# Odd tokens of two batches by quadrants in a later phase, and another order of work between two batches

## The chip, the cores and the metric

The kernel runs on one core of a Trainium2 chip. The metric is the device time of one execution in microseconds. A core has TensorE (PE, matrix products; its weight loads are listed as PEld), VectorE (DVE), ScalarE (ACT), GpSimd (POOL) and SyncE (SP, which issues DMAs), each with its own instruction queue, on-chip memory of 128 partitions (SBUF), and accumulator banks for matrix products (PSUM).

## The reference

Linear attention over 8 batches of 8 heads with 576 tokens of 64 dimensions, followed by a two-layer network over the 4608 tokens.

```python
def _attn_ref(q, k, v):                       # 8 x 8 x 576 x 64
    phi = lambda x: np.where(x > 0, x, np.exp(x) - 1.0) + 1.0
    q_p, k_p = phi(q), phi(k)
    kv = np.einsum('bhsd,bhse->bhde', k_p, v)
    z = np.sum(k_p, axis=2)
    num = np.einsum('bhsd,bhde->bhse', q_p, kv)
    den = np.einsum('bhsd,bhd->bhs', q_p, z)[..., None] + 1e-06
    return num / den

def _moe_ref(x, w_in, w_out, beta):           # x: 4608 x 512, w_in: 512 x 2048, w_out: 2048 x 512
    h = x @ w_in
    g = h * (1.0 / (1.0 + np.exp(-beta * h)))
    return g @ w_out
```

## The kernel before

Everything is bf16 on TensorE with f32 accumulation. Each engine's instructions run in the order in which the program writes them; the order is fixed by hand, and tiles with a tag rotate through a fixed number of buffers (`bufs`), so that a new tile waits for the readers of an old one.

**Tokens.** A batch's 576 tokens are 64 groups of J = 9. Slot j of every group makes a row of 64 tokens, and four pairs of slots make four blocks of 128 tokens (t = 0 to 3). Slot 8, the odd one, is block 4 and has only 64 tokens per batch. The odd tokens of all eight batches are gathered in `xT_tail` (512 tokens) and go through the network as a ninth batch at the very end.

**Phases.** For each batch b there is an h phase (Hb: 16 blocks `ff` of 128 hidden units, each with four matmuls of 512 columns, `h_mm`, L395, followed by the swish on ScalarE, `silu`, L403) and a y phase (Yb: four tiles of 128 tokens with 16 matmuls each, `y_mm`, L413, copied out of PSUM by VectorE and stored by DMAs of SP, `y_out`). The loop over b = 1 to 8 at the end of the program puts side work into these phases with `at(phase, place, ...)`: the attention of batch b+1 into Hb (`kv_both` at ff 10, `numers` and `norms` after ff 15), its transposition into Yb's queue (`x_trans_dma`), the feature map of batch b+2 into Yb (`phi_all`, `q_trans_dma`), and loads. Batch 0 and the part of batch 1 ahead of H1 are written out in straight code, because nothing precedes them to hide them.

**Batches 2 to 7** form keys times values, and the sums of keys as a 65th column of the values, by quadrants (`kv_both`, L224): four products of 64x64 in the four quarters of the PE array. `numers` (L289) multiplies the transposed queries with it in the same way; the queries are transposed by DMA (`q_trans_dma`), and so is the result x (`x_trans_dma`).

**Batches 0 and 1** before the change: the sums of the keys (`z_products`) and keys times values (`kv_direct`) go through `row_products` (L179), products with 64 rows and all 128 columns in two row halves, of which the mask keeps the diagonal blocks (`z_evac` L190, `kv_evac` L203, `diagonal` L616). Queries are transposed on TensorE (`q_trans`, L257). Denominators are small matmuls of two columns (`dens`, L475), with `recips` (L482) on VectorE; numerators are `numer_mm` (L563) and `numer0` (L493), normalised into a tile `xs`, which TensorE transposes (`x_part` L587, `x_trans` L371) and ScalarE or VectorE copies into `xT` or `xT_tail`. The odd block of batch 0 is spread over H0 (transposition at ff 5, denominators at ff 7, numerators at ff 8, x at ff 10); that of batch 1 is computed with the other blocks, and its x is transposed at ff 8 of H1.

**Between H0 and H1** stands Y0, written by hand: its matmuls (`y_mm(0, t, i, ...)`, i = quarter of the hidden units) fill TensorE between the steps of batch 1's attention. `w_out_scale` (VectorE, L668) must have scaled the quarter i of `w_out` before.

**Loads.** POOL issues the loads that convert from f32 to bf16, one behind the other: keys and values of batch 0, four parts of `w_in`, `w_out` and the inputs of batches 1 and 2 in the order of the program. SP issues all other DMAs, the transposing ones among them.

Of the kernel before, what the change touches and what calls it, by code (L numbers as in the profile page):

```python
# [16 lines left out]
def kernel(  # L17
# [79 lines left out]
    tiny = consts.tile([P, 2], BF16)  # L97
    nc.scalar.activation(tiny[:, 0:1], warm[:, 0:1], ACTF.Exp)
# [76 lines left out]
    def row_products(b, pr, dsts, mov):  # L175
        for j in range(J):
            for hh in range(2):
                r = slice(hh * G, (hh + 1) * G)
                nc.tensor.matmul(  # L179
                    dsts[hh], st[b, "k"][r, pr, j, :], mov(r, j),  # L180
                    start=(j == 0), stop=(j == J - 1), skip_group_check=True,
                )

    def z_products(b, pr, ps):

        row_products(b, pr, [a[:, 256 + 2 * pr : 258 + 2 * pr] for a in ps], lambda r, j: ones[r])

    def z_evac(ps):
        for hh in range(2):
            nc.vector.tensor_mul(  # L190
                z0[:, hh], ps[hh][:, 256:260].rearrange("p (a h) -> p a h", a=2),
                kvmask[:, :, :, 0],
            )

    def kv_direct(b, pr, ps):
        row_products(
            b, pr, [a[:, pr * P : (pr + 1) * P].rearrange("p (h d) -> p h d", h=2) for a in ps],
            lambda r, j: vb[b][r, 2 * pr : 2 * pr + 2, j, :],
        )

    def kv_evac(b, hh, prs, ps):
        p0, p1 = prs[0], prs[-1] + 1
        nc.vector.tensor_mul(  # L203
            st[b, "kv"][:, hh, p0:p1].rearrange("p a (h e) -> p a h e", h=2)[:, :, :, 0:D],
            ps[hh][:, p0 * P : p1 * P].rearrange("p (a h d) -> p a h d", a=p1 - p0, h=2),
            kvmask[:, p0:p1, :, 0:D],
        )
# [7 lines left out]
    def kv_both(b):  # L215

        t = num_tile("kvp")
        for pr in range(2):
            for j in range(J):
                for h in range(2):  # L220
                    for hh in range(2):
                        r = slice(hh * G, (hh + 1) * G)
                        c = slice(h * D, (h + 1) * D)
                        nc.tensor.matmul(  # L224
                            t[c, hh, pr * EA : (pr + 1) * EA],
                            st[b, "k"][r, pr, j, c],
                            vaug[b % 2][r, pr, j, h, 0:EA],
                            start=(j == 0), stop=(j == J - 1), skip_group_check=True,
                        )
        st[b, "kvd"] = work.tile([P, 2, 2 * EA], BF16, tag="kv_bd", name="kvd")  # L230
        nc.vector.tensor_copy(st[b, "kvd"], t[:, :, 0 : 2 * EA])  # L231
# [16 lines left out]
    def q_trans(b, ts, tp, engs):  # L248

        if (b, "qT") not in st:  # L250
            st[b, "qT"] = work.tile([P, NT, 2, 2, P], BF16, tag="qT", name="qT")
# [12 lines left out]
    def q_trans_dma(b):  # L264
        st[b, "qTd"] = work.tile([P, 38, G], BF16, tag="qT", name="qTd")
        nc.gpsimd.memset(st[b, "qTd"][:, 36:37], 0.0)
        for hh in range(2):
# [3 lines left out]
            )  # L271

# [29 lines left out]
    def numers(b):  # L302
# [9 lines left out]
        st[b, "nps"] = pairs, odd  # L312

# [47 lines left out]
    def x_trans(b, t, eng):  # L361
        n = P if t < NT - 1 else G
        xv = st[b, "xs", t].rearrange("p i a d -> p (i a d)")
        if b == 1 and t == NT - 1:
            tp = num_tile("xtp")[:, 0].bitcast(BF16)[:, 0 : KC * P].rearrange(
                "p (c t) -> p c t", c=KC
            )
        else:
            tp = miscps.tile([P, KC, P], BF16, tag="misc", name="xtp")
# [10 lines left out]
    def x_trans_dma(b, t):  # L380
# [5 lines left out]
        for pr in range(2):  # L386
            nc.sync.dma_start_transpose(
                out=xT_tail[:, pr:4:2, b * G : (b + 1) * G],
# [128 lines left out]
    for i in range(3):  # L517
        load_w_out(i)
    load(nc.gpsimd, xk[1], k, 1)
    load(nc.gpsimd, xq[1], q, 1)  # L520
# [29 lines left out]
    z_evac(zt)  # L550

    def q_trans0(t):
        q_trans(0, (t,), misc_bf()[:, 0 : 512 if t < NT - 1 else 256], (nc.scalar,))
# [58 lines left out]
    def diagonal(hh):  # L612

        for h in range(2):
            r = slice(h * D, (h + 1) * D)
            nc.scalar.copy(  # L616
                kv0[r, hh, 1, h * EA : h * EA + D], kvp0[hh][r, P + h * D : P + (h + 1) * D]
# [29 lines left out]
    for ff in range(4, FC):  # L647
# [3 lines left out]
        if ff == 5:  # L651
            q_trans0(4)
        if ff == 7:
            dps4 = num0_tile()
            dens(0, (4,), dps4)
            recips(4, 5, G, dps4)
        if ff == 8:
            numer0(0, 4)
        if ff == 10:
            x_trans(0, 4, nc.vector)  # L660
# [18 lines left out]
    yps = [mm_tile("y_ps") for _ in range(4)]  # L679
    phi_all(1, "k")  # L680
    phi_all(1, "q")
# [4 lines left out]
    kv_tile(1)  # L686
    y_mm(0, 0, 2, yps[0])
    y_mm(0, 1, 2, yps[1])
    for pr in range(2):
        z_products(1, pr, kv1)  # L690
    z_evac(kv1)
    w_out_scale(3, 0)
    y_mm(0, 2, 2, yps[2])
    for ts in ((0, 1), (2, 3)):
        q_trans(1, ts, num0_tile().bitcast(BF16), (nc.scalar, nc.scalar))
    y_mm(0, 3, 2, yps[3])
    dps1 = num0_tile()
    q_trans(1, (4,), dps1.bitcast(BF16)[:, 512:768], (nc.scalar,))
# [4 lines left out]
    dens(1, range(NT), dps1)  # L703
    recips(0, 4, P, dps1)
    recips(4, 5, G, dps1)
# [30 lines left out]
    numer0(1, 4)  # L736
# [36 lines left out]
    for b in range(1, B + 1):  # L773
        n = b + 1
        sh, sy = {}, {}
        if b == 1:
            at(sh, 0, lambda: q_trans_dma(2))
            at(sh, 8, lambda: x_trans(1, 4, nc.vector))
            at(sh, 1, lambda: [v_copy(nc.gpsimd, 2, pr) for pr in range(2)])
            at(sh, 2, lambda: load_kq(3, st[2, "qTd", "dma"]), lambda: load_v(3))  # L780
        if n < B:
# [42 lines left out]
```

## Time and profile before

| | |
|---|---|
| median of 4 runs | 289.35 us (288.54 to 291.07) |
| the profiled execution | 291.07 us, span 289.3 us |
| PE busy | 278.4 us, 96% |
| ACT busy | 159.9 us, 55% |
| DVE busy | 107.4 us, 37% |
| POOL busy | 37.1 us, 13% |
| DMA | 40.90 MB, mean 141 GB/s |

Times in the trace count from the start of the span. The first h matmul starts at 15.02, H0 ends at 33.26 with the first matmul of Y0, H1 starts at 53.17, Y1 at 68.95, H2 at 82.94. A line of the timeline merges neighbouring instructions of one kind: start, busy time, engine, line, operation, tiles, shape, count, and in brackets the idle time ahead of it with what ended it. Matmuls overlap, so the distance from one start to the next tells the cost of a group better than its busy time. Some matmul records are missing from the trace.

### The profile page before, as it was taken

To read this page: it belongs to the slowest core of one execution; us is meant where nothing else is said; L and a number is where in the kernel's file an instruction comes from. 1 tells how busy PE (TensorE), PEld (TensorE's weight loads), DVE (VectorE), ACT (ScalarE), POOL (GpSimd) and SP (SyncE) were. 2 spreads that over 40 slices of the span, in tenths; PEclk is the share of its full clock that TensorE was granted. 3 is DMA by queue.
4 is the path that set the end of the run, shared out by engine and by line. 5 is a ranking of instruction groups with operands and counts; after the bars stand their busy time and mean duration, and the time that the engine had idled before them with its cause. 6 is when DMAs were issued, how large, how long until landed. Compare 5 with 4: busy or idle time off the path is not lost.

```text
span 289.3 us, 5761 instructions
## 1 busy us (share of the span) xinstructions
PE 278.4 (96%) x2374; PEld 138.6 (48%) x2409; DVE 107.4 (37%) x261; ACT 159.9 (55%) x217; POOL 37.1 (13%) x54
## 2 busy tenths in 40 slices
PE   7799999999999999999999999999999999999994
PEld 2594447544444444444445444544454444444443
DVE  5731866834630491038203930293026100110021
ACT  5758856965837852785177718770860076018500
POOL 8632100310005000500050006100000000000000
PEclk9979999999999999999999999999999999999999
DMA  8999999599789839983898489848404510230033
GB/s 218 205 220 381 251 252 184 129 165 243 89 144 272 159 64 149 270 154 64 130 270 163 77 130 267 164 78 113 120 2 78 116 36 0 51 85 11 0 74 75
DMA packets 51083, 40.90 MB, mean 141 GB/s; under 512 B 30944, under 2 KB 42480, under 8 KB 51056
## 3 DMA queue, kind: packets, MB, share of 16 engines
q1 hardware_dynamic: 38160, 23.48, 37.5%
q0 software_dynamic: 12736, 16.91, 29.8%
q8 instruction: 19, 0.31, 0.4%
q10 hardware_dynamic: 160, 0.13, 0.2%
q14 instruction: 8, 0.07, 0.1%
HBM read 36.71 MB, written 9.44 MB: 160 GB/s over the span
## 4 chain that ended last, share of the span: by engine, by line
PE 92%; DMA 3%; issue 1%; POOL 1%; DVE 0%; ACT 0%; POOLq 0%
PE y_ps L413 43%; PE h_ps L395 42%; DMA w_in<-in_moe_w_in_dram 3%; PE kvp L224 1%; PE h_ps L597 1%; PE nps L289 1%; PE kv L179 1%; POOL vf L83 1%; PE nps_m L289 1%; PE xtp L371 0%; PE nps L493 0%; POOL xk L83 0%; PE nps L257 0%; PE tp L587 0%; PE nps L475 0%
## 5 line engine op out<-in xcount | busy, mean ns | idle before, releaser
L403 ACT ACTIVATE g<-h_ps,beta_c 128x512 bf16<-128x512 f32 x144 | 98.0, 688 | 95.2 <-PE h_ps L395 94.7
L413 PE MATMUL y_ps<-w_out,g 128*128 128x512 bf16 (+3 forms) x583 | 125.7, 370 | 0.8
L395 PE MATMUL h_ps<-xT,w_in 128*128 128x512 bf16 x481 | 109.4, 379 | 1.1 <-DVE xT L378 0.2
L413 PEld LDWEIGHTS <-g 128*128 128x128 bf16 x600 | 57.6, 98 | 64.0
L395 PEld LDWEIGHTS <-w_in 128*128 128x128 bf16 x560 | 54.0, 98 | 63.9 <-issue 0.2
L237 DVE COPY y_sb<-y_ps 128x512 f32<-128x512 f32 (+2 forms) x35 | 23.5, 673 | 73.2 <-PE y_ps L413 73.2
L231 DVE CAST kvd<-kvp 128x260 bf16<-128x260 f32 x6 | 2.6, 429 | 50.0 <-PE kvp L224 50.0
L83 POOL DMA_DIRECT2D xq<-in_q_dram x7 | 5.2, 743 | 111.9 <-ACT g L403 75.8
L142 ACT ACTIVATE e<-xk 128x1152 bf16<-128x1152 bf16 x16 | 17.9, 1152 | 1.1 <-DMA xk<-in_k_dram 1.1
L142 ACT ACTIVATE e<-xq 128x1152 bf16<-128x1152 bf16 x14 | 15.6, 1155 | 0.1
L395 PE MATMUL h_ps<-xT_tail,w_in 128*128 128x512 bf16 x62 | 13.9, 379 | 0.1
L153 DVE TENSOR_TENSOR phi_k<-e,r 128x1152 bf16<-128x1152 bf16 x16 | 11.6, 754 | 2.4 <-ACT e L142 2.1
L319 DVE TENSOR_TENSOR xs<-nps,rden 128x512 bf16<-128x512 f32 (+1 forms) x24 | 12.2, 552 | 0.4
L153 DVE TENSOR_TENSOR phi_q<-e,r 128x1152 bf16<-128x1152 bf16 (+2 forms) x17 | 11.7, 718 | 0.7 <-ACT e L142 0.4
L328 DVE TENSOR_SCALAR den<-nps 128x12 f32<-128x12 f32 x12 | 2.0, 165 | 25.8 <-PE nps L289 25.8
L171 POOL CAST vaug<-vf 128x1152 bf16<-128x1152 f32 x10 | 11.2, 1158 | 1.6 <-DMA vf<-in_v_dram 1.6
L142 ACT ACT_TABLE_LOAD x6 | 7.7, 1283 | 2.6 <-DMA xq<-in_q_dram 2.5
L319 DVE TENSOR_TENSOR xs<-nps_m,rden 128x256 bf16<-128x256 f32 (+1 forms) x24 | 7.3, 352 | 3.3 <-DMA xT<-xs 3.0
L403 ACT ACT_TABLE_LOAD x6 | 7.7, 1283 | 0.1
L131 PE MATMUL warm_ps<-xT 128*128 128x512 bf16 x19 | 6.2, 479 | 1.6 <-DVE xT L96 1.5
L83 POOL DMA_DIRECT2D xk<-in_k_dram x9 | 6.8, 751 | 3.2 <-DMA g<-in_moe_w_out_dram 2.0
L146 DVE TENSOR_SCALAR r<-xk 128x1152 bf16<-128x1152 bf16 x16 | 6.7, 452 | 0.3 <-DMA xk<-in_k_dram 0.3
(86 smaller groups left out, 126.1 us busy)
## 6 DMA issues: line engine op xcount, KB each, us to landing
out_dram<-y_sb SPq DMA_DIRECT2D x70, 128.0 KB, 2.4
vf<-in_v_dram SPq DMA_DIRECT2D x5, 1152.0 KB, 6.3
xk<-in_k_dram POOLq DMA_DIRECT2D x7, 576.0 KB, 12.4
xq<-in_q_dram POOLq DMA_DIRECT2D x7, 576.0 KB, 10.2
w_in<-in_moe_w_in_dram POOLq DMA_DIRECT2D x4, 512.0 KB, 12.2
g<-in_moe_w_out_dram POOLq DMA_DIRECT2D x2, 1024.0 KB, 17.6
stage<-in_moe_w_out_dram POOLq DMA_DIRECT2D x2, 1024.0 KB, 20.6
stage<-in_q_dram SPq DMA_DIRECT2D x2, 576.0 KB, 4.1
```

Of the source, the lines that this page charges most:

```text
L83: return eng.dma_start(out=dst[:, h0 : h0 + n].rearrange("p h j d -> p h (j d)"), in_=rows.rearrange("(i p) e -> p i e", p=P)[:, h0 : h0 + n],
L131: nc.tensor.matmul(warm_ps[:, 0:cols], warm[:, 0:P], warm[:, 0:cols], start=True, stop=True)
L142: nc.scalar.activation(st[b, a, pr, "e"][:, :, j0:j1], x[:, :, j0:j1], ACTF.Exp)
L146: nc.vector.tensor_scalar(r, x, 0.0, 1.0, ALU.max, ALU.add)
L153: nc.vector.tensor_tensor(st[b, a][:, pr, j0:j1].rearrange("p j (h d) -> p j h d", h=2), st[b, a, pr, "e"][:, :, j0:j1].rearrange("p h j d ...
L171: eng.tensor_copy(vaug[b % 2][:, pr, :, :, 0:D], src[:, places(b, pr)].rearrange("p h j d -> p j h d"))
L237: eng.tensor_copy(dst, src)
L289: nc.tensor.matmul(dst[h][c * G : (c + 1) * G, e * EA : (e + 1) * EA], st[b, "qTd"][r, (hh * 2 + p) * J + j, :], st[b, "kvd"][r, hh, p * E ...
L319: nc.vector.tensor_mul(out, num, rd[..., None].to_broadcast(list(num.shape)))
L395: nc.tensor.matmul(hp[:, c0:c1], w_in_sb[ff // 4][:, kc, (ff % 4) * P : (ff % 4 + 1) * P], x[:, kc, c0:c1], start=(kc == 0), stop=(kc == K ...
L403: nc.scalar.activation(g_sb[b % 2][:, ff, :], hp, ACTF.Silu, scale=beta_c[:, ff : ff + 1])
L413: nc.tensor.matmul(yp[:, c0:c1], g_sb[b % 2][:, ff, t * P : (t + 1) * P], w_out_sb[i][:, c, c0:c1], start=(ff == 0), stop=(ff == FC - 1), ...
```

## The change

The sums of the keys and keys times values of batches 0 and 1 go by quadrants, through a function `k_quads` that `kv_both` now uses too. The sums are also written into the 65th columns of `kv` by a copy on POOL. The odd block of batches 0 and 1 loses its denominators, numerators and transposition in H0, in the stage ahead of H1, and in H1; only its queries are transposed on TensorE as before, into tiles of their own (`q_odd_trans`). At ff 10 of H2 `odd_numers` computes the odd tokens of both batches by quadrants, `odd_norms` normalises them, and at ff 11 four transposing DMAs of SP put them into `xT_tail`. Batch 1's queries are loaded ahead of its keys and are mapped and transposed first; its sums and its keys times values follow one another, after three quarters of Y0 instead of around them. The last slots of `qTd` with their memset on POOL are gone.

```diff
+    def k_quads(b, pr, dst, mov):
         for j in range(J):
-            for hh in range(2):
-                r = slice(hh * G, (hh + 1) * G)
-                nc.tensor.matmul(
-                    dsts[hh], st[b, "k"][r, pr, j, :], mov(r, j),
-                    start=(j == 0), stop=(j == J - 1), skip_group_check=True,
-                )
+            for h in range(2):
+                for hh in range(2):
+                    r = slice(hh * G, (hh + 1) * G)
+                    c = slice(h * D, (h + 1) * D)
+                    nc.tensor.matmul(
+                        dst[hh][c], st[b, "k"][r, pr, j, c], mov(r, j, h),
+                        start=(j == 0), stop=(j == J - 1), skip_group_check=True,
+                    )
...
-        row_products(b, pr, [a[:, 256 + 2 * pr : 258 + 2 * pr] for a in ps], lambda r, j: ones[r])
+        k_quads(b, pr, [a[:, 256 + pr : 257 + pr] for a in ps], lambda r, j, h: ones[r, 0:1])
...
+        nc.gpsimd.tensor_copy(
+            st[b, "kv"].rearrange("p x a (h e) -> p (x a h) e", h=2)[:, :, D],
+            z0.rearrange("p x a h -> p (x a h)"),
+        )
...
     def q_trans_dma(b):
-        st[b, "qTd"] = work.tile([P, 38, G], BF16, tag="qT", name="qTd")
-        nc.gpsimd.memset(st[b, "qTd"][:, 36:37], 0.0)
+        st[b, "qTd"] = work.tile([P, 4 * J, G], BF16, tag="qT", name="qTd")
...
+    def q_odd_trans(b, tp):
+        tv = tp.rearrange("p (a n) -> p a n", a=2)
+        for pr in range(2):
+            nc.tensor.matmul(
+                tv[:, pr], st[b, "q"][:, pr, J - 1, :], identity,
+                is_transpose=True, start=True, stop=True, skip_group_check=True,
+            )
+        nc.scalar.copy(
+            q_odd[b].rearrange("p (i a) g -> p a i g", i=2),
+            tv.rearrange("p a (i g) -> p a i g", i=2),
+        )
...
+    def odd_numers():
+        dst = num_tile("nps_o")
+        for b in range(2):
+            for hh in range(2):
+                for pr in range(2):
+                    for h in range(2):
+                        r = slice(h * D, (h + 1) * D)
+                        e = 2 * b + hh
+                        nc.tensor.matmul(
+                            dst[pr * G : (pr + 1) * G, h, e * EA : (e + 1) * EA],
+                            q_odd[b][r, 2 * hh + pr, :],
+                            st[b, "kv"][r, hh, pr, h * EA : (h + 1) * EA],
+                            start=True, stop=True, skip_group_check=True,
+                        )
+        st["odd"] = dst
+
+    def odd_norms():
+        nv = st["odd"][:, :, 0 : 4 * EA].rearrange("p h (n e) -> p h n e", e=EA)
+        den = work.tile([P, 2, 4], F32, tag="den", name="den")
+        rden = work.tile([P, 2, 4], F32, tag="rden", name="rden")
+        nc.vector.tensor_scalar(den, nv[:, :, :, D], 1e-6, None, ALU.add)
+        nc.vector.reciprocal(rden, den)
+        for b in range(2):
+            x = xs_tile(b, 4)[:, 0:4].rearrange("p (h n) d -> p h n d", h=2)
+            n = slice(2 * b, 2 * b + 2)
+            scale(x, nv[:, :, n, 0:D], rden[:, :, n])
...
+    load(nc.gpsimd, xq[1], q, 1)
     load(nc.gpsimd, xk[1], k, 1)
-    load(nc.gpsimd, xq[1], q, 1)
...
         if ff == 5:
-            q_trans0(4)
-        if ff == 7:
-            dps4 = num0_tile()
-            dens(0, (4,), dps4)
-            recips(4, 5, G, dps4)
-        if ff == 8:
-            numer0(0, 4)
-        if ff == 10:
-            x_trans(0, 4, nc.vector)
+            q_odd_trans(0, misc_bf()[:, 0:256])
...
+    phi_all(1, "q")
     phi_all(1, "k")
-    phi_all(1, "q")
...
     kv_tile(1)
+    q_trans(1, (0, 1), num0_tile().bitcast(BF16), (nc.scalar, nc.scalar))
     y_mm(0, 0, 2, yps[0])
     y_mm(0, 1, 2, yps[1])
+    q_trans(1, (2, 3), num0_tile().bitcast(BF16), (nc.scalar, nc.scalar))
+    w_out_scale(3, 0)
+    y_mm(0, 2, 2, yps[2])
+    y_mm(0, 3, 2, yps[3])
+    dps1 = num0_tile()
+    q_odd_trans(1, dps1.bitcast(BF16)[:, 512:768])
     for pr in range(2):
         z_products(1, pr, kv1)
-    z_evac(kv1)
-    w_out_scale(3, 0)
-    y_mm(0, 2, 2, yps[2])
-    for ts in ((0, 1), (2, 3)):
-        q_trans(1, ts, num0_tile().bitcast(BF16), (nc.scalar, nc.scalar))
-    y_mm(0, 3, 2, yps[3])
-    dps1 = num0_tile()
-    q_trans(1, (4,), dps1.bitcast(BF16)[:, 512:768], (nc.scalar,))
+    z_evac(1, kv1)
     for pr in range(2):
         kv_direct(1, pr, kv1)
...
-    dens(1, range(NT), dps1)
+    dens(1, range(4), dps1)
     recips(0, 4, P, dps1)
-    recips(4, 5, G, dps1)
...
-    numer0(1, 4)
...
-            at(sh, 8, lambda: x_trans(1, 4, nc.vector))
...
+        if b == 2:
+            at(sh, 10, odd_numers, odd_norms)
+            at(sh, 11, lambda: [x_trans_dma(i, 4) for i in range(2)])
```

## The prediction

> **What bounds the kernel now.** I read the page's head first, then the chain that ended last, then TensorE's timeline around every place that the change touches, then the clock and the queues.
>
> ```profile
> span 289.3 us, 5761 instructions
> PE 278.4 (96%) x2374; PEld 138.6 (48%) x2409; DVE 107.4 (37%) x261; ACT 159.9 (55%) x217; POOL 37.1 (13%) x54
> PE 92%; DMA 3%; issue 1%; POOL 1%; DVE 0%; ACT 0%; POOLq 0%
> ```
>
> TensorE is 92% of the chain; the 3% of DMA is the wait for the first part of `w_in` (5.22 to 14.97). From 20 us on a nanosecond taken from TensorE's queue counts in full unless the queue then meets a wait; a nanosecond taken from another engine counts nothing. So the sum is one over TensorE instructions, with a search for the next wait. The timeline of H0 (batch 0's h phase):
>
> ```profile
> 23.52 1.89 PE L395 MATMUL h_ps<-xT,w_in 128*128 128x512 bf16 x8
> 25.34 0.29 PE L475 MATMUL nps<-z,qT 128*64 128x2 bf16 x4
> 25.56 1.04 PE L395 MATMUL h_ps<-xT,w_in 128*128 128x512 bf16 x4
> 26.52 0.42 PE L493 MATMUL nps<-kv,qT 128*64 128x128 bf16 x4
> 26.88 1.90 PE L395 MATMUL h_ps<-xT,w_in 128*128 128x512 bf16 x8
> 28.71 0.29 PE L371 MATMUL xtp<-identity,xs 64*128 64x64 bf16 x4
> 28.93 4.49 PE L395 MATMUL h_ps<-xT,w_in 128*128 128x512 bf16 x19
> ```
>
> Columns: start, busy us, engine, line, operation, tile, count. The next line of this view (y_ps L413) starts at 33.26; 20 matmuls lie between it and 28.93 (5 of 16 blocks; one record is missing), so one 512-column matmul takes 4.33/20 = 0.2165 us. The stage between the batches and H1:
>
> ```profile
> 41.99 0.60 PE L179 MATMUL kv<-ones,phi_k 64*128 64x2 bf16 x36
> 42.52 1.04 PE L413 MATMUL y_ps<-w_out,g 128*128 128x512 bf16 x4
> 45.37 1.18 PE L179 MATMUL kv<-vf,phi_k 64*128 64x128 bf16 x36
> 46.48 0.77 PE L475 MATMUL nps<-z,qT 128*128 128x2 bf16 x20
> 47.18 1.04 PE L413 MATMUL y_ps<-w_out,g 128*128 128x512 bf16 x4
> 52.59 0.42 PE L493 MATMUL nps<-kv_bd,qT 128*64 128x128 bf16 x4
> 53.17 7.93 PE L395 MATMUL h_ps<-xT,w_in 128*128 128x512 bf16 x35 [0.16 <-DVE xT L378]
> 61.26 1.90 PE L395 MATMUL h_ps<-xT,w_in 128*128 128x512 bf16 x8
> 63.09 0.78 PE L224 MATMUL kvp<-vaug,phi_k 64*64 64x65 bf16 x72
> 63.80 4.49 PE L395 MATMUL h_ps<-xT,w_in 128*128 128x512 bf16 x19
> ```
>
> The reader is to see that TensorE has work all the way, that H1's start is set by VectorE's last copy to `xT` and not by TensorE, and that `kv_both` shows the price of quadrants: 72 in 63.80 - 63.09 = 0.71 us, with an entry of 63.09 - (61.26 + 8 x 0.2165) = 0.10 us.
>
> **H0, removed: 1.08 us.** Odd tokens of batch 0 lose 4 denominators, 4 numerators and 4 transposes. From 23.52 to 28.93 there are 5.41 us for 20 big matmuls (4.33), so the three small groups and their changes of tile shape cost 5.41 - 4.33 = 1.08. The two transposes of q stay (q_odd_trans has the same two). VectorE loses the odd blocks' work, which was off the path.
>
> **Batch 0's sums and kv by quadrants: 0.** They lie before 15.02, where the first h matmul waits for `w_in` (landed 14.97). Cover: the chain to it goes through 0.17 us of idle, so a slowdown of the 36+36+36+36 quadrants beyond about 0.2 us would show; the bounds are -0.1 and +0.3.
>
> **Middle: 0.40 + 0.28 us.** Before, z costs 0.10 entry + 0.53 (42.52 - 41.99), kv 0.10 + 1.11 (46.48 - 45.37): 1.84. After, one run: entry 0.10, kv 0.62 (0.71 less the way out), z, and 0.10 out. 72 quadrants with one column stand nowhere in the trace. Upper bound: 0.71, what 72 with 65 columns take; lower: 0.44, because the four tiles overlap and 36 row pairs took 0.53 with their way out. I take 0.62, nearer to the quadrant row, because a weight load stays with each. After: 1.44, so 0.40 is saved (0.3 to 0.6). The denominators go from 20 to 16: the four of the half-width tile cost 0.22 + 0.10 alone in H0; here I take 0.28. The four numerators at 52.59 save **nothing**: H1 waits for VectorE's copy (52.70 to 53.12) whether they stand there or not.
>
> [...]
>
> **H1, removed: 0.32 us**, four 64x64 transposes, as at 28.71 (0.22 + 0.10 entry). **H2, added: 0.16 us**, 16 quadrants at 0.71/72, in the same run as `kv_both`, so with no entry of their own. Bounds 0.13 and 0.3.
>
> **Other queues.** VectorE: odd_norms is four small instructions in H2, where VectorE is nearly idle (1.12 of 14.6 us). POOL: the two copies of z are 128x8 and stand ahead of the loads of batch 2; the first comes to its turn at 21.04, when POOL waits until 22.91 for a landing anyway, so it moves no load. The memsets of `qTd` go, at POOL's idle time. ACT: same count of copies. SP: four more transposing DMAs in H2 (below).
>
> **What is met next.** The loads land in one file, by the trace's landings: batch 1's first at 33.94, the second at 36.83, `w_out` 3 at 39.45, v1 at 42.13, q2 at 44.98; these do not move with TensorE. With q first: y starts at 33.26 - 1.08 = 32.18 and needs q transposed after 32 matmuls, at 39.1. ACT: table load to 34.4, exp of q to 36.6, VectorE's min to 37.4: in time by 1.7 us. exp of k from 36.83 to 39.05, phi_k at 39.8, `w_out` 3 scaled at 41.5; z stands at 43.5 and y's last quarter at 45.3. v1 at 42.13 against 44.1. q2's exp is wanted near 46.9, landed 44.98. Nothing is late, so the gain goes through. In Y1 the next margin is smaller: the third output tile needs a PSUM buffer that VectorE frees at about 75.2, and TensorE wants it at 68.95 + 32 x 0.2165 = 75.9; what it waits for is a transposing DMA behind the loads, which moves by 1.8 where TensorE moves by 2.1, so 0.7 shrinks to 0.4.
>
> **Sum:** 1.08 + 0.40 + 0.28 + 0.32 - 0.16 = 1.92 us. The profiled execution took 291.07 for a span of 289.3 (1.8 around it): 289.15. It is 1.72 above the median of the four, so on the median 289.35 - 1.92 = 287.4. A measurement of this kernel tells about 1% (2.9 us) from no change.
>
> **Rivals.**
>
> *A. The clock decides (faster side).* The windows around the front, columns us, busy of five engines, granted clock, DMA, GB/s:
>
> ```profile
> 11.60:15.00 3.40, 2.69 (x69) 2.04 (x65) 2.41 (x10) 2.47 (x8) 1.48 (x2) 0.99 1.24 207
> 15.00:18.40 3.40, 3.38 (x33) 3.39 (x34) 1.11 (x4) 1.36 (x5) 1.28 (x2) 0.51 1.25 208
> ```
>
> One stretch of 3.4 us runs at half clock after a thin one (2.69 of 3.40 busy with small matmuls). Without it up to 3.38/2 = 1.7 us go: 285.7. With another: 289.1. The quadrants make that stretch thinner, if anything, and the runs of before already spread by 2.5 us. By these rows alone the stretch stays where it is and costs both kernels the same. [...] Chance 0.17.
>
> *B. The middle gives nothing* (z by quadrants at far more than its bound, a stall for instructions in 288 of them in a row; the trace has such a wait of 0.48 in the nps_m quadrants at 127.5): 0.68 lost, 0.5 more: 288.6. Chance 0.2.
>
> *C. x by DMA (slower).* In H2 SP issues four transposes while the loads of batch 4 run (86.95 to 100.05). VectorE's and SP's timelines at Y2, and a line of the waits (us in total, times, longest):
>
> ```profile
> 102.19 0.49 DVE L319 TENSOR_TENSOR xs<-nps_m,rden 128x128 bf16<-128x128 f32 x2 [0.17 <-DMA xT<-xs]
> 99.12 5.87 SPq L383 DMA_TRANSPOSE xT<-xs  x4
> DVE xs L319 <- DMA xT<-xs: 3.0, 4, 2.2
> ```
>
> They hold xs buffers 1 and 2, and batch 3's xs and its transposes stand behind. A transpose behind loads took 5.05 us against 2.4 free (first of Y1: 69.85 to 74.90). VectorE frees the odd PSUM tiles at 102.6, y's third tile wants one at 98.23 + 6.93 = 105.2: the cover is 2.6 us, and beyond it the cost is one to one. Free of each other, the four would be issued from 91.9 on, 1.4 apart, and land by 98.8, before xs 3 wants its buffer (99.1): cost 0. With every issue at 2.3 us and every landing 5 late, the last xs waits to about 105.3, 5 us late: 2.4 beyond the cover, which gives back the gain (289.9). To end clearly slower the file must be 8 us late, about 292.5. Chance 0.10, most of it near 290.
>
> **How the numbers follow.** Forecast 0.53, A 0.17, B 0.2, C 0.10. The forecast's own range is 286.4 to 288.6 (bounds of the steps +-0.4, spread of the runs before +-0.7); I take it up to 289.8, which holds B and most of C, and down to 285.5, which holds A. Under 286.5 lies most of A and a little of the forecast, 0.21; above 292.2 a part of C and of the unforeseen, 0.05.
>
> **What would show it.** Right: no small group between the h matmuls of H0 but two transposes; y of batch 0 begins 1.1 us earlier, H1 1.8, H2 2.1; z and kv as one run of 144 quadrants of 1.2 to 1.4 us; 0.6 to 0.7 us idle ahead of H1; VectorE's xs of batch 3 without a wait over 1 us. Wrong: a wait of TensorE for phi_q or phi_k between 39 and 45, z over 0.8 us, Y1's or Y2's third tile waiting for VectorE, or a different number of half-clock stretches.

## The result and the profile after

| | before | after |
|---|---|---|
| median | 289.64 us (64 runs, 288.21 to 292.92, and one of 418.16) | 289.96 us (43 runs, 288.56 to 292.03) |
| ratio | | 1.0008, 95% interval 0.9995 to 1.002 |
| the profiled execution | 291.07 us, span 289.3 | 289.89 us, span 288.1 |

The change makes no difference that these runs can tell: the predicted 1.9 us are not there. A ratio, here and below, compares two sets of executions as a whole and need not be the quotient of their medians. In the profiled executions TensorE runs at half clock (granted 0.50) from 14.94 to 18.36 (before, 3.42 us) and from 12.53 to 19.36 (after, 6.83 us, twice that), and the mean granted clock is 0.992 and 0.988. In other executions of both kernels it is 1.000; where that matters, the text counts the "full-clock" executions, those with a mean of 0.996 or more. Where the lost clock lies is known only for executions with a trace.

The page of after, its head, the shares of its chain and the row of the granted clock (40 slices of 7.2 us); the last fence is the clock row of before:

```profile
span 288.1 us, 6035 instructions
...
PE 278.0 (96%) x2511; PEld 138.4 (48%) x2545; DVE 106.4 (37%) x257; ACT 160.3 (56%) x217; POOL 36.3 (13%) x50
...
PEclk9869999999999999999999999999999999999999
...
q8 instruction: 20, 0.33, 0.4%
...
PE 93%; DMA 2%; DVE 1%; issue 1%; ACT 1%; POOLq 0%; DVEq 0%
```

```profile
PEclk9979999999999999999999999999999999999999
```

TensorE bounds both. The page holds 273 TensorE instructions more (2511 + 2545 against 2374 + 2409), yet PE is busy for 0.4 us less. Slices 2 and 3 of the clock row are lower than before. The row q8 is a stream of instructions: 20 transfers of 16 KB (0.33 MB) beside TensorE's 5056 recorded instructions, so about 253 to a transfer (19 for 4783 before, 252). It is read as TensorE's because it follows TensorE's count: 19 transfers in the pages with up to 5010 recorded instructions (e7), 20 in those with 5056 and more. This row, which the prediction passed over, matters below.

TensorE's timeline of after, at the front, at H0, at the stage between the batches, and at H2 (columns as before; the counts x6 at 32.55 and x1 at 52.59 end with the view's window):

```profile
16.35 1.03 PE L633 MATMUL h_ps<-xT,w_in 128*128 128x128 bf16 x8 [0.37 <-issue]
...
22.08 1.89 PE L434 MATMUL h_ps<-xT,w_in 128*128 128x512 bf16 x7
23.80 0.28 PE L280 MATMUL tp<-identity,phi_q 128*128 128x128 bf16 x2
23.91 8.80 PE L434 MATMUL h_ps<-xT,w_in 128*128 128x512 bf16 x40
32.55 1.67 PE L452 MATMUL y_ps<-w_out,g 128*128 128x512 bf16 x6
...
44.01 0.74 PE L183 MATMUL kv<-ones,phi_k 64*64 64x1 bf16 x72
45.10 0.83 PE L183 MATMUL kv<-vf,phi_k 64*64 64x64 bf16 x72 [0.36 <-DVE z L194]
45.86 0.55 PE L514 MATMUL nps<-z,qT 128*128 128x2 bf16 x16
...
50.36 0.83 PE L452 MATMUL y_ps<-w_out,g 128*128 128x256 bf16 x6 [0.16 <-issue]
...
52.59 0.38 PE L434 MATMUL h_ps<-xT,w_in 128*128 128x512 bf16 x1 [0.51 <-DVE xT L417]
...
91.48 0.26 PE L339 MATMUL nps_o<-kv,q_odd 64*64 64x65 bf16 x8
91.57 0.23 PE L339 MATMUL nps_o<-kv_bd,q_odd 64*64 64x65 bf16 x8
...
97.88 0.22 PE L305 MATMUL nps_m<-kvd,qTd 64*64 64x65 bf16 x4 [0.32 <-issue]
```

H0 is clean: two transposes and h matmuls. The middle is one run as foreseen, but with a wait of 0.36 inside it. And at 16.35, 50.36 and 97.88 TensorE waits for "issue": for nothing that the profile shows of another engine.

How long each stage lasts on TensorE, start to start, from the profiled executions (the first column is H0's start, counted from its first matmul of 512 columns, because the pieces of 128 columns ahead of it lie between the steps of batch 0's attention; Y0 includes the wait ahead of H1; "rest" is from Y3 to the end). H2 of before starts at 82.78 in its trace, not at 82.94:

| kernel | H0 at | H0 | Y0 | H1 | Y1 | H2 | Y2 | H3 | rest |
|---|---|---|---|---|---|---|---|---|---|
| before | 21.68 | 11.58 | 19.91 | 15.78 | 13.83 | 15.45 | 13.83 | 16.12 | 161.12 |
| after | 22.08 | 10.47 | 20.04 | 15.48 | 13.82 | 16.15 | 13.82 | 15.48 | 160.78 |
| before + fifth buffer (e16) | 19.78 | 11.57 | 19.91 | 15.78 | 13.83 | 15.45 | 13.82 | 15.73 | 161.13 |
| odd tokens alone + fifth buffer (e15) | 20.03 | 10.47 | 19.66 | 15.57 | 13.83 | 15.73 | 13.82 | 15.65 | 160.80 |

H0 gains 1.11 and H1 0.30, as predicted. In this pair of executions they are partly spent on H0's later start (0.40), to Y0 (0.13 longer, not 0.68 shorter) and to H2 (0.70 longer, not 0.16). This pair flatters the change: before's profiled execution was 1.4 above its median.

VectorE and SP of after around Y2, the place of rival C:

```profile
99.85 1.02 DVE L363 TENSOR_TENSOR xs<-nps,rden 128x512 bf16<-128x512 f32 x2 [0.78 <-DMA xT_tail<-xs]
...
101.83 1.15 DVE L363 TENSOR_TENSOR xs<-nps_m,rden 128x256 bf16<-128x256 f32 x4 [0.56 <-DMA xT_tail<-xs]
```

```profile
92.75 5.44 SPq L426 DMA_TRANSPOSE xT_tail<-xs  x4
```

The four transposes are issued between 92.75 and 96.96 and land by 101.7; batch 3's xs waits 1.34 us for them, and Y2 is as long as before (13.82): hidden.

### The profile page after: what moved, and what is told of

Its sections match the earlier page's. It is cut to its first block, busy times and chain, and to the rows that moved or that the text cites. A ratio compares the mean times of both kernels' runs of the same rounds, so it can differ in the third digit from the quotient of the medians.

```text
span 288.1 us, 6035 instructions
## 1 busy us (share of the span) xinstructions
PE 278.0 (96%) x2511; PEld 138.4 (48%) x2545; DVE 106.4 (37%) x257; ACT 160.3 (56%) x217; POOL 36.3 (13%) x50
## 4 chain that ended last, share of the span: by engine, by line
PE 93%; DMA 2%; DVE 1%; issue 1%; ACT 1%; POOLq 0%; DVEq 0%
PE y_ps L452 43%; PE h_ps L434 42%; DMA xk<-in_k_dram 2%; PE h_ps L633 2%; PE kvp L183 1%; PE nps L305 1%; PE kv L183 1%; PE nps_m L305 1%; DVE phi_k L154 1%; PE tp L623 1%; PE nps L599 0%; ACT e L143 0%; PE nps L532 0%; PE xtp L410 0%; PE nps L261 0%
## 5 line engine op out<-in xcount | busy, mean ns | idle before, releaser
L183 PEld LDWEIGHTS <-phi_k 64*64 64x64 bf16 x720 | 7.2, 109 | 4.1 <-issue 3.0
```

Source lines behind the costliest of these rows:

```text
L183: nc.tensor.matmul(dst[hh][c], st[b, "k"][r, pr, j, c], mov(r, j, h), start=(j == 0), stop=(j == J - 1), skip_group_check=True,)
```

## The experiments

Each kernel ran beside the kernel before on its chip; "n of m" counts full-clock executions. For after they are 8 of 44, for before 103 of 134.

### Which part loses the gain

**e1_odd_only.** The odd tokens' move alone, with 16 denominators instead of 20; batches 0 and 1 keep row halves and the old order.

```diff
-        z_products(1, pr, kv1)       # quadrants
+        z_rows(1, pr, kv1)           # row halves, as before; kv likewise,
+                                     # in batch 0 too; k loaded ahead of q
```

> The odd tokens' move alone: odd numerators of batches 0 and 1 by quadrants in H2 with x by DMA; sums and keys times values of both batches stay row halves, and batch 1's keys stay first. Theory 'clock' (the quadrants of batch 0 thin out the start, a second half-clock stretch follows in many executions and eats what was gained later): -1.5 us against before (1.1 in H0, 0.3 denominators, 0.3 in H1, less 0.2 in H2), and as much full clock as before. Theory 'supply' (the longer program of TensorE makes it stall for instructions, which eats the gain): this program is hardly longer than before, so also about -1.5, with stalls as before. Theory 'DMA' (x by DMA in H2 or the loads take the gain back): 0 +-0.5.

289.48 against 289.97, ratio 0.9981 (0.9948 to 1.0014), 8 of 12. H0, Y0, H1 and H2 of its profile are 10.47, 19.62, 15.47 and 15.64, so the steps are there (1.0 us in the span), yet the median has half a microsecond. The interval, -1.5 to +0.4 us, holds both the expected -1.5 and no gain.

**e4_no_odd.** The complement: quadrants and order as in after, odd tokens as in before.

```diff
+            q_trans(0, (4,), misc_bf()[:, 0:256], (nc.scalar,))   # ff 5; dens, numer0
+            x_trans(0, 4, nc.vector)                              # and x at 7, 8, 10
-            at(sh, 10, odd_numers, odd_norms)
```

> The other half of the change alone: sums and keys times values of both batches by quadrants, batch 1's queries first, z and kv in one run; the odd tokens are handled as before in H0, before H1 and in H1. Clock: slower than before by 0.7 to 1.2 us (the middle about 0, half of the executions with a second half-clock stretch). Middle alone: +0.1 to +0.3. Supply: +0.3 to +0.8, seen as stalls of TensorE beside no change in the clock.

292.33 against 289.97, 1.0062 (1.0034 to 1.009), 4 of 12. So the other half of the change costs time instead of giving 0.40, and more than any theory expected (at most 1.2). Its profile has waits of 0.55 and 0.38 at the instructions that are looked at below (446 and 1214), and half clock from 13.76 to 20.59 (mean granted clock 0.988). The halves do not add up: -0.5 (e1) and +2.4 stand against +0.3 for the whole, and the runs do not settle where the rest goes.

**e10_front_quads.** Before, with only batch 0's sums and kv by quadrants: the step that the prediction priced at 0.

```diff
-    z_products(0, 0, zt)
+    z_quads(0, 0, zt)                # batch 0 only; kv_quads likewise
```

> The kernel before with one edit: batch 0's sums and keys times values by quadrants. The prediction's step: 0 (-0.1 to +0.3). Front theory (the quadrants cost a stall for an instruction block near 16 us and full clock): +1.0 to +1.8 against before, a stall of 0.4 to 1.7 us ending 2.0 to 2.5 us after a fetch that begins near 14, H0 starting at 21.2 or later, full-clock share under half. If only the clock: +0.5 to +0.8 and no stall.

290.35 against 289.83, 1.0027 (1.0003 to 1.005), means 0.78 apart, 4 of 12. Less than the expected 1.0 to 1.8, but not 0. Its timeline:

```profile
15.71 0.42 PE L624 MATMUL tp<-identity,xs 128*128 128x128 bf16 x2
16.60 1.03 PE L634 MATMUL h_ps<-xT,w_in 128*128 128x128 bf16 x8 [0.47 <-ACT xT L628]
```

TensorE stands still in the thin part of the front, and eight 128-column products take 1.03 us (granted clock 0.50 from 15.0 to 18.4) where they take 0.61 at full clock (e15, 1.00). Half clock lasts from 13.82 to 20.64 here, 6.8 us against 3.4 in before's profile, and H0 starts at 22.76 against 21.68. These are two losses, looked at one by one below.

**e2_front_rows.** After, with batch 0 back to row halves.

```diff
-    z_products(0, 0, zt)
+    z_rows(0, 0, zt)                 # batch 0 only; kv_rows likewise
```

> The changed kernel with batch 0's sums and keys times values as row halves again; all else changed. Clock: -1.2 to -1.5 us against before and against the changed kernel; granted clock of the executions like before's, mostly one half-clock stretch (0.994) or none. Middle (z by quadrants and the wait for z's evacuation lose the gain): the same as the changed kernel, about +0.2 against before. Supply: half of the added instructions are gone, -0.4.

A miss: 292.33 against 289.97, 1.0074 (1.0047 to 1.0102), 0 of 12. In its profile the front ran at full clock (no slice of the clock row under 9 tenths up to 43.6 us), as the clock theory wanted, but the stall moved into batch 1's kv, and was longer:

```profile
43.90 0.82 PE L183 MATMUL kv<-vf,phi_k 64*64 64x64 bf16 x70 [0.35 <-DVE z L194]
46.67 0.26 PE L183 MATMUL kv<-vf,phi_k 64*64 64x64 bf16 x2 [1.96 <-issue]
```

70 quadrants run, then TensorE waits 1.96 us ahead of the last two. Clock records show half clock from 46.0 to 52.8 behind it (6 and 8 tenths in slices 7 and 8 of the page's clock row). An instruction transfer begins at 44.30 in this trace, 2.37 us before the wait ends.

### The supply of instructions

Counting weight loads and matmuls in the program's order, such waits end at instruction 446 and 1214 in after, 958 in e2, 2236 (97.88) in after and 2490 in before. In order they are 512, 256, 1022 and 254 apart, so within 2 of multiples of 256, near the 253 to a transfer (records are missing from some traces, so that a count can be off by a few). In all of them a 16 KB transfer began 2.2 to 2.6 us before the wait ended (after: 14.03, 48.05, 95.59). The wait of 0.47 in e10 ends at 446 too, 2.5 us after a transfer's start, though the profile puts it down to ScalarE.

**e6_shift** and **e12_shift16.** After, with 64 and 32 instructions that do nothing useful put at the front, so that the same boundaries meet other work.

```diff
     idle(15)
+    idle(32, 2)                      # 32 two-column products; e12: idle(16, 2)
```

> The changed kernel with 32 matmuls of two columns (64 instructions) behind the first warming matmuls, in time that TensorE waits: they only shift where in its program the blocks of instructions begin. Supply: the stall near 16.4 us, 2.3 us after a fetch at 14.0, changes its place or size by more than 0.3 us, and so may the one at 50.4; every stall of over 0.3 us not ended by another engine still ends 2.2 to 2.5 us after a fetch begins. Clock alone: stalls and time as in the changed kernel.

> The changed kernel with half of the shift, 16 matmuls of two columns (32 instructions). Supply: neither the 289.9 of no shift nor the 293.5 of 64 instructions by necessity; the stall near 16 us stands at the same number of instructions from the program's start (about 446), which now lies inside or just behind batch 0's second quadrants, so it grows: 290.5 to 292.5. Without supply: 289.9 +-0.3.

e6: 293.54 against 290.0, 1.0122 (1.0093 to 1.0151), 0 of 6. e12: 292.0 against 289.83, 1.0071 (1.0044 to 1.0098), 0 of 6. The waits of e6, then of e12 (one of which the profile puts down to ScalarE):

```profile
15.93 0.43 PE L183 MATMUL kvp<-vf,phi_k 64*64 64x64 bf16 x15 [2.47 <-issue]
...
51.42 0.57 PE L532 MATMUL nps<-kv_bd,qT 128*128 128x128 bf16 x7 [1.64 <-issue]
```

```profile
15.83 0.39 PE L624 MATMUL tp<-identity,xs 128*128 128x128 bf16 x2 [1.72 <-ACT kv L653]
...
51.64 0.29 PE L532 MATMUL nps<-kv_bd,qT 128*128 128x128 bf16 x2 [1.22 <-issue]
```

In after the first wait stood ahead of h_ps (L633); here it stands ahead of kvp and of tp, each again instruction 446, and the second again 1214; e6 has a third, of 0.70, at 72.71, again 2.2 us after a transfer's start. So the place belongs to the position in the program, not to a tile or to an engine.

**e7_rows_shift.** e2 with the same 64 instructions.

```diff
-    z_products(0, 0, zt)
+    z_rows(0, 0, zt)                 # as e2
+    idle(32, 2)                      # as e6
```

> The kernel with batch 0 by row halves and the rest changed, which ran at 292.3 with a stall of 2.1 us inside the run of 144 quadrants, plus the same 64 instructions in front. Supply: the stall of 2.1 us goes or falls under 1, with it the half clock at 46 to 53, and the time falls by 1.5 to 3 us to 289 to 290.5. Clock or middle: no change, 292 +-0.5.

289.2 against 290.0, 0.9961 (0.9937 to 0.9986), 8 of 12: 3.1 us below e2 by instructions that compute nothing. Its profile has no such wait; TensorE waits 1.73 us for `w_in` there, ahead of its first h matmul.

**e3_fill.** After, with z ahead of y's last products of that stage, so that these lie between z and kv.

```diff
+    for pr in range(2):
+        z_products(1, pr, kv1)
+    z_evac(1, kv1)
     y_mm(0, 3, 2, yps[3])
```

> The changed kernel with batch 1's z moved ahead of the last third-quarter y matmuls and of the odd queries' transposition, so that keys times values no longer follow z at once and the wait of 0.36 us for VectorE's z is covered; two more changes of tile shape (0.2). Middle: -0.2 against the changed kernel. Clock: the same -0.2 and no more, so still no faster than before by 0.5. If the wait were worth nothing: +0.2 against the changed kernel.

289.79 against 289.97, 0.9983 (0.9948 to 1.0018), 5 of 12. The wait of 0.36 for z_evac goes, and Y0 is 19.33 against after's 20.04; the front's stall of this profile is larger:

```profile
16.86 0.62 PE L633 MATMUL h_ps<-xT,w_in 128*128 128x128 bf16 x8 [1.56 <-issue]
```

**e11_before_shift.** Before, with the 64 instructions.

```diff
     idle(15)
+    idle(32, 2)
```

> The kernel before plus the 64 shifting instructions in front, nothing else. Supply: a time that differs from before by 0.3 to 2 us in either direction, with stalls in other places of the trace. Clock or other reasons alone: within 0.3 of before.

289.41 against 289.83, 0.9996 (0.9974 to 1.0018), 10 of 12. The supply theory expected a loss of at least 0.3 here and missed: without the quadrants of the change no wait shows in this profile. Most transfers show no such wait: three of after's 20 are followed by one (0.37, 0.16 and 0.32 us) and one of before's 19 (0.48). The waits seen stand in runs of small products or just behind them, up to 2.47 us (e6), and not every such run has one; which ones, the runs do not settle.

### The clock of the front

**e5_idle.** After, with four 512-column warming products between the front's sums.

```diff
     kv_direct(0, 0, kvp0)
+    idle(1)                          # one here, one behind beta, two behind kv's
+                                     # second half
```

> The changed kernel with four more warming matmuls of 512 columns at the start, where TensorE waits anyway (one after keys times values of the first half, one after beta's transposition, two after the second half). Theory 'clock' (the quadrants thin the start, so a half-clock stretch follows in most executions): the share of executions at full clock rises from about 1 in 5 towards the 7 in 10 of before, and the median falls by 0.5 to 1 us against the changed kernel, to about 0.7 under before. Theory 'supply' (TensorE stalls until an instruction block of 16 KB has come, some 2.3 us after its fetch begins): the clock's share may move, but the stall of 0.4 to 1.7 us near 16.4 stays, and the median moves by less than 0.4.

289.19 against 290.0, 0.9985 (0.996 to 1.0009); 10 of 12 against after's 8 of 44, and 0.8 below after's median. Before stands at 103 of 134, and e10, before with nothing but the quadrants in the front, at 4 of 12. So the quadrants cost the front its clock, and more work gives it back. That they do it by leaving TensorE with less to do (a half of kv is busy for 0.48 us where it was 0.68, a half of the sums for 0.45 where it was 0.38) fits, but was not shown by itself. The gain in time is less sure than the share: this interval and after's (0.9995 to 1.002) overlap. In e5's profile `w_in` comes later than instruction 446, so that the stall there shows no price; those at 1214 and 2236 stay (0.34 and 0.30):

```profile
17.12 0.62 PE L635 MATMUL h_ps<-xT,w_in 128*128 128x128 bf16 x8 [1.79 <-DMA w_in<-in_moe_w_in_dram]
```

### What Y1 keeps

**e8_rows_z.** e2 with batch 1's z by row halves ahead of y's last products, kv by quadrants.

```diff
+        z_rows(1, pr, kv1)
+    z_evac_rows(1, kv1)
     y_mm(0, 3, 2, yps[3])
-        z_products(1, pr, kv1)
```

> Batch 0 by row halves, batch 1's sums by row halves with y matmuls between them and keys times values, keys times values by quadrants, the odd tokens moved: what the profiles so far say is cheapest. By the sum of measured steps (1.1 in H0, 0.3 denominators, 0.3 in H1, 0.3 from keys times values, less 0.2 in H2): -1.8 us against before, if no block of instructions ends in a run of quadrants; if one does, up to 2 us worse (supply). Clock: full-clock share as before.

289.66 against 290.0, 0.998 (0.9957 to 1.0003), 8 of 12: a miss, 0.3 where 1.8 was expected. Its H0 starts at 19.77, two microseconds ahead of before's. Y0 loses 1.3 us in two waits for phi_q (shown for e13 below), and Y1 is 2.2 longer than before's: more than the lead. Y1, TensorE, then VectorE:

```profile
66.56 7.08 PE L490 MATMUL y_ps<-w_out,g 128*128 128x512 bf16 x32
75.63 7.08 PE L490 MATMUL y_ps<-w_out,g 128*128 128x512 bf16 x32 [1.99 <-DVE xs L401]
```

```profile
69.59 0.76 DVE L401 TENSOR_TENSOR xs<-nps_m,rden 128x256 bf16<-128x256 f32 x2
...
75.28 0.49 DVE L401 TENSOR_TENSOR xs<-nps_m,rden 128x128 bf16<-128x128 f32 x2 [4.93 <-DMA xT<-xs]
```

After 32 matmuls of Y1 TensorE needs a PSUM buffer. VectorE empties it into the last xs of batch 2, and waits 4.93 us for one of four xs buffers, which a transposing DMA still reads. In before's profile the same wait is 2.19 us and ends early enough that TensorE does not wait:

```profile
74.92 0.49 DVE L319 TENSOR_TENSOR xs<-nps_m,rden 128x128 bf16<-128x128 f32 x2 [2.19 <-DMA xT<-xs]
```

**e9_rows_fill_shift.** e7 with e3's order.

```diff
+    z_evac(1, kv1)                   # e7, z ahead of
     y_mm(0, 3, 2, yps[3])
```

> Batch 0 by row halves, the 64 shifting instructions in front, batch 1's z with y matmuls between it and keys times values, the rest as changed. The version with the shift alone ran 0.8 us under before, with no stall for instructions in its trace; covering the wait of 0.36 for z's evacuation at 0.2 for two more changes of tile shape should bring 0.2 to 0.4 more: -1.0 to -1.4 against before, full-clock share as before. If it stalls for instructions again (supply), 1 to 2 us worse.

289.49 against 289.83, 0.9978 (0.9957 to 1.0), 8 of 12: a miss, 0.3 where 1.0 to 1.4 were expected. TensorE waits 1.3 us in Y1.

**e13 to e16.** Four kernels with a fifth xs buffer, for which the row of betas moves into a tile that is free until batch 2: e7, e9, e1, and before as the control.

```diff
-    beta_row = consts.tile([FC, P], F32)
+    beta_row = xT[2][0:FC, 0, 0 : 2 * P].bitcast(F32)
-        xs = work.tile([P, 4, 2, D], BF16, tag="xs", name="xs", bufs=4)
+        xs = work.tile([P, 4, 2, D], BF16, tag="xs", name="xs", bufs=5)
```

> e7_rows_shift with a fifth xs buffer (the fifth KB of each partition comes from laying the row of betas into xT[2], which is not used until batch 2). Cap theory (part of the gain of H0 and H1 ends in Y1, where the third y tile waits for an xs that waits for a free buffer behind the transposing DMA): VectorE's wait of 1.7 us in Y1 goes, and the time falls below e7's 289.2 by 0.3 to 0.8, in the executions at full clock most. Rival (the cap lies elsewhere, in the clock or nowhere): the same time as e7, within 0.2, VectorE's wait gone or not.

> e9_rows_fill_shift with a fifth xs buffer. Its profile showed TensorE waiting 1.3 us in Y1 for that xs. Cap theory: the wait goes, the time falls from 289.49 to 288.2 to 288.8, and this is the fastest kernel of the study. Rival: the wait moves to the next stage (the DMA's landing itself is late, not the buffer), and the time stays at 289.2 to 289.6.

> e1_odd_only with a fifth xs buffer. e1 gained 0.5 us where its steps H0 and H1 sum to 1.3. Cap theory: 288.5 to 289.1, the missing 0.4 to 0.9 us come out. Rival (the missing part is a lower share of executions at full clock, 8 of 12): 289.3 to 289.6.

> The control: the kernel before with the fifth xs buffer. TensorE never waits for that xs in its profile, so both theories expect no change, within 0.3 us. If this one gains as much as the others, the buffer has nothing to do with the change.

| | median | without the buffer | ratio to before (289.86) | full clock |
|---|---|---|---|---|
| e13 (e7) | 287.79 | 289.2 | 0.9956 (0.9923 to 0.999) | 7 of 8 |
| e14 (e9) | 287.79 | 289.49 | 0.9934 (0.9909 to 0.996) | 6 of 6 |
| e15 (e1) | **287.41** | 289.48 | 0.9926 (0.9898 to 0.9953) | 6 of 6 |
| e16 (before) | 288.73 | 289.86 | 0.9975 (0.995 to 1.0) | 10 of 12 |

The three gain 1.4, 1.7 and 2.1 us with the buffer, more than the cap theory expected (0.3 to 0.8, 0.7 to 1.3, 0.4 to 0.9). But both theories expected no change of the control, and it gained 1.1, at the edge of its interval (0.65 between the full-clock medians, 289.32 and 288.67): so the kernel before seems to be held in Y1 too, in executions that its one profiled one (H0 at 21.68) does not show. No trace of such an execution of before was taken, and the move of the betas' row, which all four have, was not run without the buffer; that it gave a part of the gain is not ruled out. Beyond the control's gain 0.3 to 1.0 us are left. The odd move is worth 1.3 us with the buffer (287.41 against 288.73; full-clock medians 287.40 and 288.67). Without it 0.5 was measured, in an interval that holds 1.3 as well. VectorE of e15 at the same place, all four without a wait:

```profile
68.76 1.15 DVE L401 TENSOR_TENSOR xs<-nps_m,rden 128x256 bf16<-128x256 f32 x4
```

e15 is faster than both kernels. Its profile differs from the control's (table of stages above) by -1.10 in H0, -0.25 in Y0, -0.21 in H1, +0.28 in H2 and -0.33 at the end.

e13's profile shows a wait that after's does not have. Its H0 starts early too, at 19.55, and Y0 at 30.02 where after's starts at 32.55, but batch 1's q is loaded no earlier. ScalarE waits for it, and then TensorE for phi_q:

```profile
33.68 1.28 ACT L143 ACT_TABLE_LOAD   x1 [2.78 <-DMA xq<-in_q_dram]
```

```profile
38.04 0.51 PE L299 MATMUL nps<-identity,phi_q 128*128 128x128 bf16 x6 [0.77 <-DVE phi_q L154]
```

e14 has the same wait of 0.77, e2 one of 0.65, and e8 two of 0.53 and 0.77; their Y0 starts between 30.00 and 30.53. In e18, whose Y0 starts at 31.12, and in e15, which keeps the old order, there is none. e14 also has a wait for issue of 0.37 among kv's quadrants, at instruction 958.

**e17_after_xs5** and **e18_idle_xs5.** After, and e5, with the fifth buffer (and the betas' row moved as above): what is left of the whole change when Y1 does not hold it?

```diff
-        xs = work.tile([P, 4, 2, D], BF16, tag="xs", name="xs", bufs=4)
+        xs = work.tile([P, 4, 2, D], BF16, tag="xs", name="xs", bufs=5)
```

> The whole change with the fifth xs buffer. With that buffer the odd tokens' move alone measured 287.4 and the kernel before 288.7. What the rest of the change adds to 287.4 is now free of Y1. The three mechanisms together (stalls at instructions 446 and 1214 of 0.4 and 0.3, the half-clock stretches at the front, the z_evac wait of 0.36): 288.3 to 289.3, no more than 0.4 below the control's 288.7, and at full clock in under half of the executions. Rival (the cap in Y1 was all that was wrong): 286.8 to 287.4, as the prediction's -1.92 below the control's 288.7 would have it.

> e5_idle (the whole change and four warming products between the front's sums) with the fifth xs buffer. If the half-clock stretches cost 0.7 of the change, as e5 said, this one is at full clock in most executions and 0.3 to 0.8 below e17; what is left above e15's 287.4 is the stalls and the middle's run, 0.4 to 1.0: 287.8 to 288.4. Rival (the clock was not it): the same as e17 within 0.2.

e17: 290.14 against 289.66, 0.9991 (0.9961 to 1.0021), 3 of 12. e18: 289.22, 0.998 (0.9954 to 1.0006), 11 of 12. Both lie above the expectations of the three mechanisms (288.3 to 289.3 and 287.8 to 288.4), and the rival (286.8 to 287.4) is far off. The medians of the two differ by 0.9, the means by 0.4 (289.67 and 289.24): of e17's executions five lie near 288.8 and seven near 290.3. e18's profile, its fastest execution (288.38, span 286.6), has the supply's waits and the one for z_evac:

```profile
16.11 0.29 PE L601 MATMUL nps<-kv,qT 128*128 128x128 bf16 x2 [0.89 <-issue]
...
43.67 0.83 PE L183 MATMUL kv<-vf,phi_k 64*64 64x64 bf16 x72 [0.36 <-DVE z L194]
...
48.84 0.29 PE L532 MATMUL nps<-kv_bd,qT 128*128 128x128 bf16 x2 [0.40 <-issue]
```

Against e15's profile (287.32) H0 starts 0.62 later and Y0 lasts 0.62 longer. The medians of e18 and e15 are another 0.7 further apart than these two executions. The supply's waits may vary from one execution to the next, but that was not shown: one execution of each kernel has a trace.

## Why the prediction was wrong

The gain was looked for in the right place, and half the steps hold. The kernels with the fifth buffer, whose profiles show no wait of TensorE in Y1, form a chain from before to after. By medians, the odd tokens' move gives 287.41 - 288.73 = -1.3 (e15 against e16); quadrants and order in the middle cost 287.79 - 287.41 = +0.4 (e13 against e15; e13 also carries the 64 instructions); batch 0's quadrants, with the 64 instructions left out again, cost 290.14 - 287.79 = +2.35 (e17 against e13). That these make the +1.4 by which e17 stands above e16 is so by construction and confirms nothing. The sizes are loose: by the ratios to before the three steps are about -1.4, +0.9 and +1.0, in all +0.5, each known to about 1 us, and e17 ran on another chip than the rest. The signs agree: the odd move gains, the other two steps lose. With four buffers +0.3 is what is seen; what Y1 takes there from each kernel was not measured one by one.

- **H0 (1.08), H1 (0.32), denominators (0.28):** right. 1.11 and 0.30 in the stages; 16 denominators take 0.41 to the next group in e15 (43.77 to 44.18) against 0.70 for 20 before.
- **H2 (+0.16):** 0.19 to 0.28 in e1, e13 and e15, within the bounds. After's own profile adds a wait of 0.32 for issue at 97.88, in the nps_m quadrants.
- **Batch 0's quadrants at 0 (bounds -0.1 to +0.3): the step that failed most.** Alone they cost 0.5 in the median, 0.8 in the mean (e10; the interval goes from 0.1 to 1.4). Their length does no harm, as was said (the first h matmul starts at 14.32 in after, at 15.02 in before); their cost comes behind it, at instruction 446, and in the clock. How much goes to each was not separated.
- **Middle, 0.40: the second step that failed.** With the entry of 0.10, z and kv take 1.95 (44.01 to 45.86 is 1.85) against 1.84 before. z (44.01 to 44.74) and kv (45.10 to 45.86) are 0.73 and 0.76, above the bound of 0.71, where 0.62 each and 0.10 out were taken: 0.15 more. The rest is a wait of 0.36 that the prediction did not foresee: kv's products go into the PSUM tile (`kv1`) out of which VectorE still reads z. In the order before, y's matmuls stood there, and in e3, where they stand there again, the wait is gone. z's 0.73 is 10 ns a quadrant, so quadrants of one column (72) do not beat the row halves (36 in 0.53, 15 ns each, and an entry of 0.10).
- **"Nothing is late, so the gain goes through": wrong where the front is fast.** The margin of 1.7 for phi_q was too large already: ScalarE's table load waits for q's load instead of standing ahead of it (33.85 in after), and phi_q is complete at 38.15, not 37.4. Where Y0 starts at 30.0, the margin is gone and TensorE waits 0.77 us (e13, e14). So the new order is part of the +0.4 of the middle, and the prediction had named this wait as a sign of being wrong.
- **Rival B** (the middle gives nothing, with a stall for instructions): right in kind, at 0.2. It even named the wait of 0.48 in before's nps_m quadrants, but put the stall only among the 288 instructions of the middle and no clock behind it.
- **Rival A** (the clock): the argument that the stretch stays where it is and costs both kernels the same was wrong. Full clock fell from 103 of 134 executions to 8 of 44.
- **Rival C** (x by DMA): right that it is hidden; xs of batch 3 waited 1.34 us, more than the 1 us that was named as the limit, and nobody waited for it.
- **Y1's margin (0.7, shrinking to 0.4):** the place and the mechanism were right, the size not. It was measured on an execution that reached Y1 late (H0 at 21.68). At full clock H0 starts at 19.8, the DMA does not come two microseconds earlier with it, and the margin is gone: e8 waits 1.99 us, e9 1.3, and before itself gains 0.65 to 1.1 with the fifth buffer.

## What to carry to other kernels

A margin read from one profiled execution holds for that execution's clock: where the front can run faster than the profile shows, subtract the difference before calling a step free; here this held twice, for xs in Y1 and for phi_q in Y0. Count TensorE's instructions as well as their time: where small products are dense, TensorE stood still here for 0.2 to 2.5 us with nothing to wait for but, by this reading, its instructions. Quadrants for row halves doubled the instructions of batch 1's sums and keys times values and took 0.15 us off these products (0.73 + 0.76 against 0.53 + 1.11), less than the one wait of 0.36 that came with them. Before a change is dropped because nothing came out at the end, look for the buffer behind which the gain may wait: with one more xs buffer the odd tokens' move measured 1.3 us, and the kernel before was 0.65 to 1.1 faster as well.

## What the hardware showed that was not expected

- TensorE's instructions come in transfers of 16 KB (20 for 5056 recorded instructions), and where small products are dense it stood still for 0.2 to 2.5 us at a place that stays the same by count of instructions (446 and 1214 in after, e6 and e12). The waits of this kind that were followed end 2.2 to 2.6 us after a transfer's start, and their places lie within 2 of multiples of 256 instructions apart, so they are read as waits for the next transfer. Sixty-four instructions whose result nobody uses moved a kernel by 3.1 us (e2, e7).
- Quadrants in the front cost it the clock: with them 8 of 44 executions of after kept full clock, with four warming products more 10 of 12.
- The part behind the last matmul is 0.3 us shorter in every kernel with the odd tokens moved (17.64 to 17.68 us against 17.94 to 18.03 from the last y phase's start to the end; 3.9 against 4.2 from the last matmul's start). It was not followed further.
